# Weights packed on 128 partitions, 29 slots instead of 27 and a fifth kept head in a cached-attention decode kernel

## The chip, the cores and the metric

The kernel runs on one core of a Trainium2 chip. A core has the engines TensorE (PE), VectorE (DVE), ScalarE (ACT), GpSimd (POOL) and SyncE (SP), and 16 DMA engines that move data between HBM and the core's SBUF. The metric is the device time of one execution in microseconds. Before the change it is 1222.26 us, the median of three runs (1220.59 to 1224.09).

## What is computed

Eight batch rows of width 448, one token each, go through two layers. Both layers use the same weights and the same K and V cache. One layer is attention over 4096 cached positions (16 query heads, 8 K/V heads, head size 256), and then a small MLP block. The part of the reference that matters:

```python
def _A_ref(x, k_cache, v_cache, wq, wo):      # B=8, Sq=1, D=448, Hq=16, Hkv=8, Sk=4096, Dh=256
    q = (x @ wq).reshape(B, Sq, Hq, Dh).transpose(0, 2, 1, 3)
    k = jnp.repeat(k_cache, rep, axis=1)      # rep = 2
    v = jnp.repeat(v_cache, rep, axis=1)
    scores = jnp.einsum("bhqd,bhkd->bhqk", q, k) * (Dh ** -0.5)
    o = jnp.einsum("bhqk,bhkd->bhqd", _softmax(scores), v)
    return o.transpose(0, 2, 1, 3).reshape(B, Sq, Hq * Dh) @ wo
...
x = A_x
x = x + _A_ref(_layernorm(x), A_k_cache, A_v_cache, A_wq, A_wo)
x = x + _B_ref(_layernorm(x), B_w1, B_w2, B_w3, B_w4)
x = x + _A_ref(_layernorm(x), A_k_cache, A_v_cache, A_wq, A_wo)
x = x + _B_ref(_layernorm(x), B_w1, B_w2, B_w3, B_w4)
```

With one token, the shifted terms of `_B_ref` are zero, so `w1` and `w2` drop out, and what is left of it is `x1 + gelu(layernorm(x1) @ w3) @ w4`. All inputs are bf16. K and V are 134 MB in total each; K or V of one batch row and one head is 2.1 MB.

## The kernel before

**Pairs.** The work is cut into 128 pairs (layer, batch row, K/V head). One pair takes K (2.1 MB) and V (2.1 MB) of its head. K comes in two runs of 1.05 MB (`K_RUN = 2` chunks each), V in four chunks of 0.52 MB. For a pair, DVE transposes the K runs in place in blocks of 32 by 32 (L548, four per run), PE makes the scores of both query heads from each run (L571), DVE takes the maximum (L578, L580), POOL reduces it over the partitions (L582), ACT makes the exponentials (L588), DVE transposes them (L593), PE multiplies with each V chunk (L610), DVE and PE sort and scale the result (L615, L622, L629), and PE multiplies it with the output weights into `psM` (L640).

**Slots.** K and V live in one SBUF tensor `kv`, cut in `NSLOT = 27` slots of one chunk (128 partitions by 4 KB). A K run takes two adjacent slots, a V chunk one. A slot comes free when PE has read it, and the next load into it waits for that.

**K is used twice.** Both layers need the same K of a batch row. For heads 4 to 7 (`KEEP_RUNS`) the transposed K stays in its slots from layer 0 until layer 1 has used it: 4 heads by 4 slots, 16 slots at the fullest. In layer 1 such a pair loads only V. The other heads (0 to 3) load K in both layers. So 192 K runs and 512 V chunks are loaded.

**Order of the pairs.** Layer 1 of a row can start when layer 0 has ended with the MLP block for it: function `tail` (L658 adds the attention result, then a norm, `w3`, gelu, `w4`, L697, a norm, the query projection at L454, and `expand`, which writes the queries into the tile `qx` at L480). This is the turn of the row. The list `jobs` covers it with other pairs. For a middle row b the order is: layer 0 of heads 4 to 7 of b; layer 1 of heads 0 to 3 of b-1; then `MIX = 1` layer-0 pair of b+1 ahead, and after it layer-1 pairs of b with kept K in turn with further pairs ahead.

**Queues.** All loads are issued by SP in one order: the K runs of pair n, then the V chunks of pair n-1 (`V_LAG = 1`). An issue waits in order: what stands behind a waiting load waits too. The order on PE, DVE, ACT and POOL is found when the program is built: `Graph.schedule` plays the tasks with planned durations, priorities (10 times the pair's number, with small offsets) and the slot pool, and writes down one fixed order for each engine; semaphores guard it. Multi-step DVE work stands as single tasks, so that steps of the norm and gelu in `tail` stand between the transposes of K.

**Weights and x.** `x` is loaded transposed, in pieces of four elements, on 112 partitions (L386). `wq` and `w3` are laid out as 112 partitions by four rows each, since 448 = 112 x 4 (L388, L395), `wo` and `w4` on 128 partitions (L392, L397). `wo`, `w3` and `w4` are issued after the first pairs' loads. Each row's result is stored from `xT` when its layer 1 has ended (L705).

## Time and profile before

The profiled execution took 1223.6 us; its span from the first to the last instruction is 1221.7 us, with a mean granted TensorE clock of 0.541.

| what | before |
|---|---|
| median of three runs | 1222.26 us |
| profiled execution | 1223.6 us |
| its span | 1221.7 us |
| bytes moved by DMA | 483.00 MB, mean 395 GB/s |
| read from HBM | 480.32 MB |
| K loads (1.05 MB) | 192 |
| V loads (0.52 MB) | 512 |
| DVE transposes of K (L548) | 768, mean 690 ns |
| mean granted TensorE clock | 0.541 |

The page of the profile gives each engine's busy time and its share of the span, then the span in 40 equal slices of 30.5 us: a digit is the busy share of an engine in tenths, and the last row is what the DMA engines moved in GB/s. The chain that ended last follows the work back from the last instruction to what released it. A stretch's row begins with its start and end in us. Rows that name an instruction give line, engine, operation, output and inputs. `SPq` stands for SP's queue issuing a load; its length contains the time it waited.

### The profile page before, as it was taken

How to read it: one execution, taken by the hardware profiler on the slowest of the kernel's cores; microseconds unless marked ns; L12 is line 12 of the kernel's file. 1: busy time of each engine (PE TensorE's matmuls, PEld its weight loads, DVE VectorE, ACT ScalarE, POOL GpSimd, SP SyncE). 2: the span in 40 equal slices, each digit the busy share in tenths (PEclk: the TensorE clock that was granted, in tenths of full speed). 3: DMA queues.
4: the chain of work that ended last, by engine and by line, in shares of the span. 5: the costliest groups of instructions: out<-in, count | busy, mean ns of one | idle time of the engine just before them, and what ended most of it. 6: DMA issues, size and time to landing. Idle time of an engine off the chain costs nothing.

```text
span 1221.7 us, 41286 instructions
## 1 busy us (share of the span) xinstructions
PE 727.4 (60%) x18516; PEld 496.0 (41%) x18516; DVE 822.8 (67%) x2683; ACT 118.7 (10%) x305; POOL 99.3 (8%) x272
## 2 busy tenths in 40 slices
PE   2424675567645775467755676556754577545665
PEld 1212454355423553245522454235532355323544
DVE  5627757776677666677667766677667776677763
ACT  0100011011100110000110011000110011100010
POOL 0000000000000000000000001000000001000000
PEclk9755555556555555555555555555565555555555
DMA  9999999999999999999999999999999999999994
GB/s 297 411 343 413 410 410 413 385 404 411 402 415 411 400 398 414 414 397 409 398 414 410 397 411 395 414 408 398 411 387 414 412 395 399 415 414 397 406 397 165
DMA packets 106592, 483.00 MB, mean 395 GB/s; under 512 B 13264, under 2 KB 15056, under 8 KB 81616
## 3 DMA queue, kind: packets, MB, share of 16 engines
q1 hardware_dynamic: 105392, 480.37, 99.1%
q8 instruction: 145, 2.38, 0.8%
q14 instruction: 31, 0.25, 0.1%
q10 hardware_dynamic: 1024, 0.01, 0.0%
HBM read 480.32 MB, written 0.01 MB: 393 GB/s over the span
## 4 chain that ended last, share of the span: by engine, by line
DMA 74%; PE 12%; SPq 6%; DVE 5%; issue 3%; ACT 0%; POOL 0%; ACTq 0%; DVEq 0%
DMA kv<-in_A_v_cache_dram 69%; PE psS L571 5%; SPq L559 4%; PE psO L610 4%; DMA kv<-in_A_k_cache_dram 3%; DMA wo_sb<-in_A_wo_dram 2%; SPq L542 2%; DVE kv L548 2%; PE psX L692 1%; PE psX L667 1%; DVE oT L629 1%; PE psM L640 1%; PE psO L622 0%; DVE oX L615 0%; PE psX L454 0%
## 5 line engine op out<-in xcount | busy, mean ns | idle before, releaser
L548 DVE STREAM_TRANSPOSE kv<-kv 128x512 int32<-128x512 int32 x768 | 498.9, 690 | 55.2 <-DMA kv<-in_A_k_cache_dram 54.0
L610 PE MATMUL psO<-kv,pT 128*2 128x256 bf16 x4096 | 289.7, 397 | 171.7 <-DMA kv<-in_A_v_cache_dram 141.8
L571 PE MATMUL psS<-kv,qx 128*8 128x128 bf16 x8192 | 265.5, 301 | 141.2 <-DVE kv L548 111.2
L571 PEld LDWEIGHTS psS<-kv,qx 128*8 128x8 bf16 x8192 | 210.9, 119 | 172.2 <-DVE kv L548 117.3
L610 PEld LDWEIGHTS psO<-kv,pT 128*2 128x2 bf16 x4096 | 75.2, 90 | 302.1 <-DMA kv<-in_A_v_cache_dram 248.8
L588 ACT ACTIVATE p<-psS,nb 128x256 bf16<-128x256 f32 x128 | 105.6, 834 | 899.7 <-DVE nb L584 856.7
L578 DVE TENSOR_REDUCE pm<-psS 128x1 f32<-128x256 f32 x128 | 53.9, 421 | 111.8 <-PE psS L571 108.2
L640 PE MATMUL psM<-oT,wo_sb 128*128 128x1 bf16 x2048 | 87.4, 173 | 66.1 <-DVE oT L629 53.1
L615 DVE STREAM_TRANSPOSE oX<-psO 128x256 f32<-128x256 f32 x128 | 57.1, 446 | 102.2 <-PE psO L610 101.8
L582 POOL PARTITION_ALL_REDUCE gm<-pmh x128 | 45.5, 355 | 810.2 <-DVE pmh L580 577.0
L640 PEld LDWEIGHTS psM<-oT,wo_sb 128*128 128x128 bf16 x2048 | 77.1, 117 | 82.1 <-DVE oT L629 64.0
L629 DVE TENSOR_SCALAR oT<-psO,rc 64x4 bf16<-64x4 f32 x256 | 55.4, 217 | 32.6 <-PE psO L622 28.0
L597 POOL PARTITION_ALL_REDUCE db<-rsh x128 | 51.0, 399 | 282.5 <-DVE rsh L595 234.6
L593 DVE STREAM_TRANSPOSE pT<-p 128x256 bf16<-128x256 bf16 x128 | 55.7, 436 | 12.3 <-ACT p L588 10.0
L622 PE MATMUL psO<-oX,id 128*32 128x4 f32 x1024 | 37.0, 202 | 44.3 <-DVE oX L615 33.0
L622 PEld LDWEIGHTS psO<-oX,id 128*32 128x32 f32 x1024 | 28.5, 143 | 79.4 <-DVE oX L615 60.5
L584 DVE CUSTOM_DVE_ANT_0 nbx<-gm,ownneg 128x2 f32<-128x2 f32 x128 | 19.1, 149 | 27.8 <-POOL gm L582 26.6
L692 PE MATMUL psX<-hT,w_sb 128*128 128x1 bf16 x896 | 31.7, 171 | 8.4 <-DVE hT L684 6.8
L692 PEld LDWEIGHTS psX<-hT,w_sb 128*128 128x128 bf16 x896 | 30.3, 116 | 10.9 <-DVE hT L684 9.1
L667 PE MATMUL psX<-n,w_sb 112*128 112x1 bf16 x896 | 26.2, 165 | 12.9 <-DVE n L751 12.9
L588 ACT ACTIVATION_READ_ACCUMULATOR p<-psS,nb 128x1 f32 x128 | 33.8, 264 | 0.0
L454 PE MATMUL psX<-n,wq_sb 112*128 112x1 bf16 x1024 | 29.3, 165 | 4.5 <-DVE n L751 3.2
(109 smaller groups left out, 317.1 us busy)
## 6 DMA issues: line engine op xcount, KB each, us to landing
kv<-in_A_v_cache_dram SPq DMA_DIRECT2D x512, 512.0 KB, 15.4
kv<-in_A_k_cache_dram SPq DMA_DIRECT2D x192, 1024.0 KB, 15.5
wq_sb<-in_A_wq_dram SPq DMA_DIRECT2D x1, 3584.0 KB, 17.7
wo_sb<-in_A_wo_dram SPq DMA_DIRECT2D x1, 3584.0 KB, 27.9
w_sb<-in_B_w_dram SPq DMA_DIRECT2D x2, 1568.0 KB, 30.2
out_dram<-xT ACTq DMA_DIRECT2D x8, 0.9 KB
xT<-in_A_x_dram SPq DMA_DIRECT2D x1, 7.0 KB, 2.2
```

Of the source, the lines that this page charges most:

```text
L548: return e.transpose(ap, ap)
L571: last = e.matmul(S[32 * j:32 * j + 8, w * y:w * y + w], qx[x][:, h, 2 * c + u, :], kt[:, :, c, 8 * j:8 * j + 8, u], start=(c == 0 and u = ...
L578: g.add("dve", lambda e: e.tensor_reduce(pm[par][:, :], S[:, 0:256], axis=AX.X, op=ALU.max), 0.44, pr, reads=[rS], writes=[res(f"pm{par}")])
L588: g.add("act", lambda e: e.activation(p_sb[par][:, :].rearrange("p (z k y) -> p y z k", z=8, k=8), S[:, 0:256].rearrange("p (y z k) -> p y ...
L593: g.add("dve", lambda e: e.transpose(pT[par][:, :], p_sb[par][:, :]), 0.44, pr, reads=[rP], writes=[rPT])
L597: g.add("pool", lambda e: e.partition_all_reduce(db[par][:, :], rs2[par][:, :], P, ReduceOp.add), 0.45, pr + 1, reads=[res(f"rsh{par}")], ...
L610: last = e.matmul(O[32 * j:32 * j + 2, 0:DH], pt[:, i, 2 * a:2 * a + 2], slot_ap(vin)[:, i * DH:(i + 1) * DH], start=(a == 0 and i < 4), s ...
L615: g.add("dve", lambda e: e.transpose(oX[par][:, :].rearrange("p (c r) -> p c r", r=32), O[:, 0:DH].rearrange("p (a r k) -> p a k r", a=2, ...
L622: last = e.matmul(O[32 * a:32 * a + 32, 256:260], id4[:, :], oX[par][:, :].rearrange("p (a k r) -> p a k r", a=2, k=4)[:, a % 2, :, a // 2 ...
L629: g.add("dve", lambda e, j=j: e.tensor_scalar(oT[64 * j:64 * j + 64, jb, 4 * h:4 * h + 4], O[64 * j:64 * j + 64, 256:260], rc[par][64 * j: ...
L640: last = e.matmul(psM[layer][:, c:c + 1], wo_sb[:, c0:c0 + 509:4], oT[:, jb, kt_:kt_ + 1], start=(first and k == 0 and c == 0), stop=False ...
L692: last = e.matmul(M[:, 64 + c:65 + c], w4_sb[:, c0:c0 + 509:4], hT[:, ft:ft + 1], start=(ft == 0), stop=(ft == NFT - 1))
```

## The change

- `wq` and `w3` are packed: rows 0 to 383 as three blocks of 128 partitions, and the last 64 rows in two halves of their columns, on partitions 0 to 63 and 64 to 127. Each such tensor is loaded by five transfers instead of one. The normed vectors get a fifth column: the last 64 elements a second time, on the upper partitions. `wo`, `w4` and all vectors go from 112 to 128 partitions, the fourth column filled for 64 partitions only.
- The memory saved, with one `qx` for layer 0 instead of two, and one tile each for `p` and `oX` instead of two, gives `NSLOT = 29`.
- K of five heads (3 to 7) is kept. 176 K runs are loaded.
- `MIX = 2`: at the turn two pairs of the next row come before the first layer-1 pair. With heads 0 to 2 loaded twice, a middle row is: five layer-0 pairs, three layer-1 pairs of the row before, two ahead, one layer-1 pair, one ahead, four layer-1 pairs.
- x is loaded as 8 rows into `wo_sb`, and transposed by four matmuls with an identity `eye`; the load of `wo` waits for these. The results are transposed back in the end by four matmuls, copied by ACT, and stored by one transfer.
- The planned durations become pairs (until a result can be used, and how long the engine is taken), so the fixed orders differ on all engines.

The core of the diff:

```diff
-NSLOT = 27
-KEEP_RUNS = {4: 2, 5: 2, 6: 2, 7: 2}
+NSLOT = 29
+KEEP_RUNS = {3: 2, 4: 2, 5: 2, 6: 2, 7: 2}
...
-MIX = 1
+MIX = 2
...
-BYTES_PER_US = 0.412e6
+V_RATE = 0.4096e6
+K_RATE = 0.4194e6
...
-        self.dur = dur
+        self.dur, self.occ = dur if isinstance(dur, tuple) else (dur, dur)
...
-                        free_at[e] = now + dur
+                        free_at[e] = now + got.occ
...
-    wq_sb = sb("wq_sb", [CP, NCC, HQ * DH], bf)
-    wo_sb = sb("wo_sb", [P, 32 * D + 64], bf)
-    w3_sb = sb("w3_sb", [CP, NCC, F], bf)
-    w4_sb = sb("w4_sb", [P, NFT * D + 64], bf)
+    wq_sb = sb("wq_sb", [P, 7 * HQ * DH // 2], bf)
+    wo_sb = sb("wo_sb", [P, 32 * D], bf)
+    w3_sb = sb("w3_sb", [P, 7 * F // 2], bf)
+    w4_sb = sb("w4_sb", [P, NFT * D], bf)
...
-    qx = [sb(f"qx{i}", [P, HKV, 8, 8], bf) for i in range(4)]
+    qx = [sb(f"qx{i}", [P, HKV, 8, 8], bf) for i in range(3)]
...
-    p_sb = [sb(f"p{i}", [P, 256], bf) for i in range(2)]
+    p_sb = sb("p", [P, 256], bf)
...
-    oX = [sb(f"oX{i}", [P, DH], f32) for i in range(2)]
+    oX = sb("oX", [P, DH], f32)
...
-    dma(lambda e: e.dma_start(xT[:, :, :], A_x[:, 0, :].rearrange("b (p c) -> p b c", c=NCC)),
-        8000, 0, writes=[res("xT")])
-    dma(lambda e: e.dma_start(wq_sb[:, :, :], A_wq.rearrange("(p c) n -> p c n", c=NCC)),
-        D * 4096 * 2, 0, writes=[res("wq")])
+    dma(lambda e: e.dma_start(wo_sb[0:B, 0:D], A_x[:, 0, :]), 8000, 0, writes=[res("wo")])
+
+    def packed(w_sb, w, n, name, queue):
+
+        for c in range(3):
+            dma(lambda e, c=c: e.dma_start(w_sb[:, c * n:(c + 1) * n], w[c * P:(c + 1) * P, :]),
+                P * n * 2, 0, queue, writes=[res(name)])
+        for u in range(2):
+            dma(lambda e, u=u: e.dma_start(w_sb[64 * u:64 * u + 64, 3 * n:3 * n + n // 2],
+                                           w[3 * P:D, u * n // 2:(u + 1) * n // 2]),
+                32 * n * 2, 0, queue, writes=[res(name)])
+
+    packed(wq_sb, A_wq, HQ * DH, "wq", dma_order)
+
+    def xin(e):
+        for c in range(NCC):
+            m = min(P, D - c * P)
+            last = e.matmul(psX[0][0:m, 128 + B * c:128 + B * c + B], wo_sb[0:B, c * P:c * P + m], eye[0:B, 0:B],
+                            start=True, stop=True)
+        return last
+    g.add("pe", xin, 0.5, -5, reads=[res("wo"), res("const")], writes=[res("psX0", True)])
...
-    dma(lambda e: e.dma_start(w3_sb[:, :, :], B_w3.rearrange("(p c) n -> p c n", c=NCC)),
-        D * F * 2, 0, late, writes=[res("w3")])
+    packed(w3_sb, B_w3, F, "w3", late)
...
+    def packed_ap(w_sb, n, c, f, m=P):
+
+        if c < 3:
+            return w_sb[:, c * n + f:c * n + f + m], c
+        u = f // (n // 2)
+        f = 3 * n + f - u * n // 2
+        return w_sb[:, f:f + m], 3 + u
...
-        x = 2 * layer + b % 2
+        x = layer + layer * (b % 2)
...
-        ops.append(lambda e: e.tensor_scalar(dsts[-1], xc[:, :, :], y[:, k - 1:k], None, ALU.mult))
-        g.add("dve", ops, 0.205 * len(ops), prio, reads=[rM, rL], writes=[rL, dst_res])
+        ops.append(lambda e: e.tensor_scalar(dsts[-1][:, :, 0:4], xc[:, :, :], y[:, k - 1:k], None, ALU.mult))
+        ops.append(lambda e: e.tensor_copy(dsts[-1][64:128, :, 4:5], dsts[-1][0:64, :, 3:4]))
+        g.add("dve", ops, (0.21, 0.12), prio, reads=[rM, rL], writes=[rL, dst_res])
...
-        else:
-            g.add("act", lambda e: ("dma", e.dma_start(
-                out[b, 0, :].rearrange("(p c) -> p c", c=NCC), xT[:, b, :])), 0.1, prio, reads=[nx2])
...
+    def xout(e):
+        for c in range(NCC):
+            m = min(P, D - c * P)
+            last = e.matmul(psX[0][0:B, 64 + c * P:64 + c * P + m], xT[0:m, :, c], eye[0:m, 0:m],
+                            start=True, stop=True)
+        return last
+    g.add("pe", xout, 0.5, -1, reads=[res(f"xT{b}") for b in range(B)] + [res("const")], writes=[rM])
+    g.add("act", lambda e: e.copy(wq_sb[0:B, 0:D], psX[0][0:B, 64:64 + D]), 0.6, -1, reads=[rM], writes=[res("wq")])
+    g.add("act", lambda e: ("dma", e.dma_start(out[:, 0, :], wq_sb[0:B, 0:D])), 0.1, -1, reads=[res("wq")])
```

## The prediction, made before the changed kernel had run

> **What bounds the kernel now.** I read the page first: busy time, the slices, the chain, the transfers.
>
> ```profile
> PE 727.4 (60%) x18516; PEld 496.0 (41%) x18516; DVE 822.8 (67%) x2683; ACT 118.7 (10%) x305; POOL 99.3 (8%) x272
> ...
> DMA  9999999999999999999999999999999999999994
> GB/s 297 411 343 413 410 410 413 385 404 411 402 415 411 400 398 414 414 397 409 398 414 410 397 411 395 414 408 398 411 387 414 412 395 399 415 414 397 406 397 165
> ...
> DMA 74%; PE 12%; SPq 6%; DVE 5%; issue 3%; ACT 0%; POOL 0%; ACTq 0%; DVEq 0%
> ...
> kv<-in_A_v_cache_dram SPq DMA_DIRECT2D x512, 512.0 KB, 15.4
> kv<-in_A_k_cache_dram SPq DMA_DIRECT2D x192, 1024.0 KB, 15.5
> ```
>
> No engine is busy for more than 67%, the DMA engines are busy in every slice but the last, and three quarters of the chain are transfers. Second, stages, as stretches of the trace (first busy times by engine; the last two numbers are the busy share of the DMA engines and what they moved in GB/s):
>
> ```profile
> 0.00:10.00 10.00, 0.00 (x0) 0.00 (x0) 3.20 (x11) 0.00 (x0) 1.03 (x8) 1.00 0.90 204
> 10.00:20.00 10.00, 1.62 (x25) 1.47 (x26) 3.81 (x23) 0.00 (x0) 1.92 (x8) 1.00 0.92 267
> 60.00:70.00 10.00, 1.73 (x48) 1.65 (x48) 0.00 (x0) 0.00 (x0) 0.00 (x0) 0.50 1.04 259
> 70.00:80.00 10.00, 0.00 (x0) 0.00 (x0) 0.00 (x0) 0.00 (x0) 0.00 (x0) 0.50 1.05 350
> ...
> 230.00:240.00 10.00, 5.75 (x130) 3.79 (x125) 7.10 (x26) 0.83 (x2) 0.75 (x2) 0.50 0.94 368
> 240.00:250.00 10.00, 5.21 (x140) 3.66 (x136) 7.90 (x33) 0.83 (x2) 0.75 (x2) 0.50 0.96 370
> 530.00:560.00 30.00, 20.19 (x535) 14.80 (x524) 23.39 (x90) 2.71 (x7) 2.09 (x6) 0.50 1.01 398
> 1060.00:1070.00 10.00, 5.07 (x120) 2.88 (x120) 7.07 (x19) 0.83 (x2) 0.75 (x2) 0.50 1.02 413
> 1205.00:1221.00 16.00, 6.25 (x150) 5.26 (x150) 5.38 (x30) 0.21 (x1) 0.00 (x0) 0.50 0.01 2
> ```
>
> 413 GB/s (1060 to 1070) is the rate at which DMA is full. The reader is to see four places below it: the start, while wq_sb loads; 60 to 80, while wo_sb and w3_sb load; small dips where pairs stream K and V with few slots (230 to 250, 530 to 560); and 16 us at the end with hardly any transfer. The work list is therefore: bytes, the two weight stages, the dips, the end.
>
> **The change, part by part.** Sums stand against the profiled execution, 1223.6 us (span 1221.7, 1.9 around it), which lies 1.3 above the runs' median of 1222.26.
>
> *K of five heads kept.* Layer 1 reads one more head of K from SBUF in each of 8 batches: 8 x 2 runs of 1.049 MB are not loaded, 16.8 MB of 480. At 413 GB/s that is 40.6 us. With them go 16 x 4 transposes of 690 ns (L548), 44 us of an engine that isn't the bound: nothing.
>
> *Weights on 128 partitions.* Two loads over 112 partitions are slow. From 0 to 20 the DMA moved 204 and 267, 4.7 MB; at 413 from the first byte at 2 us it would be 7.4: 2.7 MB, 6.6 us. From 60 to 80 it moved 6.1 MB instead of 8.3: 5.2 us. The packed loads have forms whose rate the trace has: 128 partitions x 8 KB is K's own form. New are four pieces on 64 partitions, 0.75 MB together. Their price lies between full rate, 1.8 us, and the 112-partition rate of about 210 (60 to 80 less its full-rate part), 3.6 us; I take the slow end, since half the partitions are nearest to that row: 1.8 us lost. Sum 6.6 + 5.2 - 1.8 = 10 saved, bounds 7 and 12. The Trainium skill has a rule against these pieces: SBUF — State Buffer, Door 1: The DMA port swizzle (why `[64,N]` ≈ `[32,N]`) says that 64 adjacent partitions reach half of the 16 ports, 196 GB/s measured there; an estimate from it is 3.8 us for the pieces. No run here shows a 64-partition load yet; by the rule the sum is 0.2 lower, by full rate 1.8 higher.
>
> *x as rows, transposed on PE.* Before the first norm come four matmuls, two copies and, within it, one more DVE step: some 0.5 + 2 x 0.2 + 0.2, and POOL's identity 0.5 later: the first scores, at 29.2 now, come 2 us later. Cover: 28 slots can fill before any is reused, 28 x 0.524 MB / 0.413 = 35 us of transfers after wq_sb, then 16 us of weights. Without it: 2 us. The load of wo_sb waits for those matmuls, near 17 us; queued behind it on SP are w3_sb, w4_sb and K of pair 4, all of which reach the DMA only after 45 us. Nothing.
>
> *Two heads ahead at the turn; one qx, p and oX less.* From the last layer-0 head of a batch to the layer-1 queries the trace has 39 us:
>
> ```profile
> 964.09 0.16 DVE L658 TENSOR_TENSOR xT<-psM,xT 112x4 bf16<-112x4 f32 x1
> ...
> 1003.44 0.29 DVE L480 CAST qx<-psX 32x128 bf16<-32x128 f32 x1
> ```
>
> A pair with K and V is 4.19 MB, 10.1 us. Before, four pairs of layer 1 and one ahead cover it (51 us); now three and two: the same. Shared p and oX wait for the transpose or matmul of the pair before, under 1 us of work in a 5 us pair: nothing, at most a share of the next part.
>
> *Fewer free slots.* This is the cost. Kept K fills 20 of 29 slots: 9 are left where 11 of 27 were. Nine hold the run of K being read (2), its second run (2) and V of the pair before (4). So, in the order of the changed program, the next pair's first run waits for this pair's first scores, with 6 chunks of 0.524 MB queued behind the landing; before, 8. How long that wait is the trace shows (start, length):
>
> ```profile
> 524.38 6.34 SPq L542 DMA_DIRECT2D kv<-in_A_k_cache_dram  x2
> ...
> 526.21 0.70 DVE L548 STREAM_TRANSPOSE kv<-kv 128x512 int32<-128x512 int32 x1
> ...
> 529.31 1.02 PE L571 MATMUL psS<-kv,qx 128*8 128x128 bf16 x32
> ```
>
> K lands, DVE starts at 526.2, PE's scores end at 530.3, SP has issued at 530.7: 4.5 us. Six chunks last 6 x 1.27 = 7.6 us, so 3.1 remain queued when the new load is issued; eight left 5.6. What a load needs before it moves at rate is the fastest landing less its own bytes: 5.5 - 2.5 = 3.0 us.
>
> ```profile
> DMA to landing us min/median/max: 5.5/15.5/31.7
> ```
>
> 3.1 against 3.0: on the edge. Behind the waiting K run SP holds V of this pair and all that follows, and PE waits for that V. Price of a pair: with 5.6 left, 530 to 560 moved 398 for 413, 1.1 us for three pairs, 0.4 each; 230 to 250, where K was issued late with three chunks left, lost (1 - 369/413) x 20 = 2.1 us for two pairs, 1.1 each. The second row is the nearer: 0.7 more per pair. There are 4 such successions of K and V pairs in each of six batches, 2 in the first and 5 in the last: 31 x 0.7 = 22 us. Ends: 0, if 3.1 us suffice, and 45, at twice the row.
>
> *End.* From the last layer's L658 to the last step the chain runs without transfers:
>
> ```profile
> 1208.08 0.17 DVE xT L658
> ...
> 1218.25 0.16 DVE xT L697
> ```
>
> The change adds the shifted copy in the norm (0.2), four matmuls (0.4) and ACT's copy of 8 x 448 from PSUM; ACT's 128 x 256 takes 0.83, a 32 x 128 copy 0.26: 0.6 to 1.2. One store of 8 rows takes the place of the last of eight; the other seven were hidden. Sum +1.5, ends 0.8 and 2.5.
>
> Sum: 1223.6 - 40.6 - 10 + 1.5 + 22 = 1196.5 in the profiled execution; 1.3 less against the median: **1195**.
>
> **The rivals.** *Transfers stay back to back.* For it: 28 slots at the start, deep queues (median 15.5 us to landing) in most of a batch, and in 160 to 180, with V alone, full rate too. Then the slot term is 0 to 8, middle 5: 1178. Against it: 3.1 us on the edge of 3.0, and the dips that 11 slots show already.
>
> *A new wait, slower than before.* In the changed order, DVE takes the norm and gelu steps of the tail between the four transposes of a K run; in the worst pair eleven stand there. At about 0.19 each the answer of 4.5 us becomes 6.6, and one chunk is left where three are needed: 2.1 us idle on top of 0.7. If it were so in all 31 successions, the slot term would be 87 us and the time 1260; in half of them 54 us and 1227. It decides from 49 us of slot loss, 1.6 per succession. For it: DVE is 7 to 8 of 10 us busy in these stretches. Against: only one of four successions of a batch has that many steps between; the others have three or four.
>
> *The weights stay slow.* If the 112 partitions were not the reason for 204 to 267 GB/s (both loads also have 14 to 32 KB runs, and the start has the 8-byte pieces of x), the 10 us stay away: 1205. Against: the piece of the trace with w4_sb, 128 partitions in 896 B rows, ends the dip.
>
> **How the numbers follow.** Forecast (slots on the edge, 1186 to 1206) 0.50; transfers back to back (1172 to 1186) 0.25; weights stay slow or twice the slot loss (1206 to 1218) 0.12; slower 0.10, no change 0.03. The range leaves out the slower tail and a little below: 1174 to 1214. A difference under 0.3%, some 3.7 us, can't be told from none with this kernel; faster by more 0.87, within 0.03, slower 0.10.
>
> **What would show it.** K loads 176 instead of 192 and the first 20 us above 350 GB/s: bytes and weights right. Slices of the steady part between 385 and 400 where pairs stream K and V, and SP's waits for psS (L571 of before) longer than now: slot term right; slices at 410: the first rival. First scores near 31 us with no dip at 45 to 60: start right. More than 18 us between the last transfer and the end, or V-only stretches under 395, would show a cost that isn't in the sum; so would a slot loss outside the successions named.

## The result, and the profile after

The changed kernel takes 1212.14 us (median of four runs, 1210.78 to 1214.98) where the kernel before took 1222.58 beside it: a ratio of 0.9919, 95% interval 0.9894 to 0.9944. The prediction was 1195, so 10 us of the 27 that were forecast came; the time lies near the upper end of the stated range, 1174 to 1214. Run once more on another chip, the changed kernel took 1210.62 against 1218.66 there, a ratio of 0.9942 (0.9914 to 0.9970). The profiled execution took 1213.35 us, its span is 1211.6.

The page of the changed kernel: busy times, the rate in 40 slices, the chain by engine, and the K and V loads.

```profile
PE 785.4 (65%) x18524; PEld 561.2 (46%) x18524; DVE 801.3 (66%) x2654; ACT 120.3 (10%) x306; POOL 100.5 (8%) x274
...
GB/s 349 409 392 411 399 392 413 404 384 384 413 414 389 343 400 413 413 349 367 411 414 388 377 394 410 414 392 372 394 411 414 396 369 392 414 414 372 272 409 125
...
DMA 42%; PE 31%; DVE 17%; issue 6%; ACT 2%; SPq 1%; POOL 1%; ACTq 0%; POOLq 0%; DVEq 0%
...
kv<-in_A_v_cache_dram SPq DMA_DIRECT2D x512, 512.0 KB, 13.8
kv<-in_A_k_cache_dram SPq DMA_DIRECT2D x176, 1024.0 KB, 14.9
```

Sixteen K runs are gone, as planned. But the slices that stood at 385 to 415 now fall to 343, 349, 367 and once to 272, and the share of the chain that is transfers fell from 74% to 42%. (That share alone does not name the bound: slots_32 below, the fastest kernel of all, has 16%.) TensorE, which has the same work, is busy for 58 us more; that comes up again below.

Stretches of the changed kernel (busy times of PE, its weight loads, DVE, ACT, POOL; then clock, busy share of DMA, GB/s):

```profile
0.00:10.00 10.00, 0.00 (x0) 0.00 (x0) 3.04 (x18) 0.00 (x0) 1.21 (x9) 1.00 0.79 300
10.00:20.00 10.00, 1.55 (x8) 1.28 (x8) 2.25 (x15) 0.00 (x0) 2.22 (x9) 1.00 1.02 333
...
60.00:70.00 10.00, 3.83 (x48) 3.41 (x48) 0.00 (x0) 0.00 (x0) 0.00 (x0) 1.00 1.08 344
70.00:80.00 10.00, 3.78 (x96) 2.07 (x96) 5.78 (x12) 0.00 (x0) 0.36 (x1) 1.00 1.02 414
250.00:290.00 40.00, 31.78 (x823) 25.17 (x819) 28.77 (x113) 4.08 (x11) 3.03 (x8) 0.54 0.98 372
...
740.00:760.00 20.00, 13.76 (x320) 9.54 (x320) 11.14 (x34) 2.00 (x6) 1.91 (x5) 0.61 1.02 414
1100.00:1150.00 50.00, 31.91 (x726) 22.18 (x726) 34.76 (x136) 4.08 (x11) 3.06 (x8) 0.50 0.82 312
...
1191.00:1211.00 20.00, 10.37 (x206) 7.90 (x202) 6.49 (x34) 0.74 (x2) 0.00 (x0) 0.50 0.01 5
```

The start moves more than before (204 and 267 then), and so does the stage of `w3` (259 and 350 then). A stretch where pairs stream K and V, 250 to 290, stands at 372 (408 before), and 1100 to 1150, the last turn, at 312 (399 before). Full rate, 414, is still there at 740 to 760. The same two stretches in the kernel before:

```profile
250.00:290.00 40.00, 29.23 (x788) 21.27 (x792) 27.10 (x106) 4.10 (x11) 3.01 (x8) 0.54 1.02 408
...
1100.00:1150.00 50.00, 32.08 (x804) 22.28 (x808) 37.46 (x129) 4.05 (x11) 3.01 (x8) 0.50 1.00 399
```

**Where the time went.** The trace has the landing of every load. With deep queues, two K runs land 2.50 us apart and two V chunks 1.275 us (medians of each trace, within 0.01 wherever K comes in runs of two chunks). These distances, times 192 or 176 runs and 512 chunks, are the transfers' own time. What successive landings lie further apart than that, summed up, I call the excess. The rest is the start with the weights, and what follows the last landing. The four add up to the span:

| us | before | after | difference | forecast |
|---|---|---|---|---|
| K and V, own time | 1133.2 | 1093.2 | -40.0 | -40.6 |
| start and weights | 41.2 | 33.6 | -7.6 | -10 |
| excess | 30.9 | 65.4 | +34.5 | +22 |
| after the last landing | 16.4 | 19.4 | +3.0 | +1.5 |
| span | 1221.7 | 1211.6 | -10.1 | -27.1 |

So the bytes came out as worked out, and 12.5 of the 17 us that are missing are excess. By blocks of 16 pairs the excess was 3.4, 4.3, 3.8, 4.6, 3.7, 4.5, 3.5, 3.2 before, and is 4.2, 7.2, 8.5, 10.0, 6.8, 7.2, 7.7, 14.0 after: 1 to 5 more in every block, and 11 more in the last. The second profile of the changed kernel has an excess of 61.0; it is from a chip on which the kernel before is 4 us faster too, and that kernel has no profile there. A median that is off by 0.003 us moves the sum over 512 V chunks by 1.5 us, so an excess is good to some 3 us.

Two things stand out beside it. First, K's loads wait longer for scores. SP's waits by line, in the kernel before (us in total, times, longest):

```profile
SPq L542 <- PE psS L571: 156.0, 57, 9.4
...
SPq L559 <- PE psX L472: 11.5, 4, 5.6
```

and in the changed kernel:

```profile
SPq L573 <- PE psS L602: 188.8, 46, 6.9
...
SPq L590 <- PE psX L505: 41.9, 11, 6.3
```

K runs (L573, L542 before) wait for scores 46 times instead of 57, but 4.1 us each instead of 2.7. V chunks (L590, L559 before) wait 41.9 us instead of 11.5 behind the matmuls that write out a turn's queries (L505, L472 before); all 11 of these waits lie before 1095, none in the last turn. A wait of SP is not yet a loss, since the loads issued before it still run: K's waits for the PV matmuls (L641, L610 before) fell at the same time, from 207.1 to 111.1.

Second, the output projection, which the diff doesn't touch in count, got slow. The group in the kernel before, with the busy time and mean ns of one after the bar:

```profile
L640 PE MATMUL psM<-oT,wo_sb 128*128 128x1 bf16 x2048 | 87.4, 173 | 66.1 <-DVE oT L629 53.1 <-DMA wo_sb<-in_A_wo_dram 10.1 <-issue 2.6
```

The same work after, in its two forms, weights of 128 and of 64 columns, and both together (they overlap, and the row names the more frequent form):

```profile
L672 PE MATMUL psM<-oT,wo_sb 128*128 128x1 bf16 x1536 | 121.8, 171 | 64.7 <-DVE oT L660 59.0 <-issue 2.5 <-DMA wo_sb<-in_A_wo_dram 2.5
...
L672 PE MATMUL psM<-oT,wo_sb 128*64 128x1 bf16 x512 | 105.7, 206 | 0.0
...
L672 PE MATMUL psM<-oT,wo_sb 128*128 128x1 bf16 (+1 forms) x2048 | 165.7, 180 | 64.7 <-DVE oT L660 59.0
```

That is 165.7 us instead of 87.4, or 1.29 us per pair instead of 0.68. Three candidates, then, for the excess: the slots, the last turn, and this.

### The profile page after: what moved, and what is told of

Its sections match the earlier page's. It is cut to its first block, busy times and chain, and to the rows that moved or that the text cites. A ratio compares the mean times of both kernels' runs of the same rounds, so it can differ in the third digit from the quotient of the medians.

```text
span 1211.6 us, 41233 instructions
## 1 busy us (share of the span) xinstructions
PE 785.4 (65%) x18524; PEld 561.2 (46%) x18524; DVE 801.3 (66%) x2654; ACT 120.3 (10%) x306; POOL 100.5 (8%) x274
## 4 chain that ended last, share of the span: by engine, by line
DMA 42%; PE 31%; DVE 17%; issue 6%; ACT 2%; SPq 1%; POOL 1%; ACTq 0%; POOLq 0%; DVEq 0%
DMA kv<-in_A_v_cache_dram 35%; DVE kv L579 9%; PE psS L602 9%; PE psO L641 8%; PE psM L672 6%; DMA kv<-in_A_k_cache_dram 5%; PE psX L726 3%; DMA wo_sb<-in_A_wo_dram 2%; PE psX L488 2%; DVE oT L660 2%; ACT p L619 1%; DVE pm L609 1%; PE psO L653 1%; DVE oX L646 1%; DVE pT L624 1%
## 5 line engine op out<-in xcount | busy, mean ns | idle before, releaser
L579 DVE STREAM_TRANSPOSE kv<-kv 128x512 int32<-128x512 int32 x704 | 453.3, 687 | 49.8 <-DMA kv<-in_A_k_cache_dram 47.7
L641 PE MATMUL psO<-kv,pT 128*2 128x256 bf16 x4096 | 280.4, 396 | 88.0 <-DMA kv<-in_A_v_cache_dram 75.1
L602 PEld LDWEIGHTS psS<-kv,qx 128*8 128x8 bf16 x8192 | 202.7, 116 | 188.4 <-DVE kv L579 117.0
L672 PE MATMUL psM<-oT,wo_sb 128*128 128x1 bf16 (+1 forms) x2048 | 165.7, 180 | 64.7 <-DVE oT L660 59.0
L672 PEld LDWEIGHTS psM<-oT,wo_sb 128*128 128x128 bf16 (+1 forms) x2048 | 141.8, 110 | 97.9 <-DVE oT L660 75.8
L641 PEld LDWEIGHTS psO<-kv,pT 128*2 128x2 bf16 x4096 | 93.8, 100 | 179.7 <-DMA kv<-in_A_v_cache_dram 141.2
L653 PEld LDWEIGHTS psO<-oX,id 128*32 128x32 f32 x1024 | 26.7, 138 | 96.3 <-DVE oX L646 80.3
L726 PE MATMUL psX<-hT,w_sb 128*128 128x1 bf16 (+1 forms) x896 | 33.3, 171 | 11.8 <-issue 6.7
L726 PEld LDWEIGHTS psX<-hT,w_sb 128*128 128x128 bf16 (+1 forms) x896 | 31.2, 113 | 17.8 <-issue 9.1
L630 DVE RECIPROCAL rc<-db 128x2 f32<-128x2 f32 x128 | 19.1, 149 | 19.4 <-POOL db L628 19.3
L611 DVE TENSOR_SCALAR pmh<-cap,pm 128x2 f32<-128x2 f32 x128 | 29.0, 227 | 3.3
```

The lines of the kernel that those rows point to most:

```text
L579: return e.transpose(ap, ap)
L602: last = e.matmul(S[32 * j:32 * j + 8, w * y:w * y + w], qx[x][:, h, 2 * c + u, :], kt[:, :, c, 8 * j:8 * j + 8, u], start=(c == 0 and u = ...
L641: last = e.matmul(O[32 * j:32 * j + 2, 0:DH], pt[:, i, 2 * a:2 * a + 2], slot_ap(vin)[:, i * DH:(i + 1) * DH], start=(a == 0 and i < 4), s ...
L653: last = e.matmul(O[32 * a:32 * a + 32, 256:260], id4[:, :], oX[:, :].rearrange("p (a k r) -> p a k r", a=2, k=4)[:, a % 2, :, a // 2], st ...
L672: last = e.matmul(psM[layer][0:m, c:c + 1], wo_sb[:, c0:c0 + m], oT[:, jb, kt_:kt_ + 1], start=(first and k == 0 and c == 0), stop=False, ...
L726: last = e.matmul(M[0:m, 64 + c:65 + c], w4_sb[:, c0:c0 + m], hT[:, ft:ft + 1], start=(ft == 0), stop=(ft == NFT - 1))
```

## The experiments

The kernel before, run beside every set, has medians from 1217.95 to 1218.67 in the five sets (1222.58 beside the result above), so times of different sets can stand beside each other. Where a difference to the changed kernel is given, it is to the 1210.62 of its run in the fourth set.

### The last turn, the output projection, three more slots, four heads

**turn_2**: one pair less behind the last turn.

```diff
         jobs += [(0, b, h) for h in range(HKV) if h in KEEP_RUNS]
-        if b:
+        if b == B - 1:
+            jobs.insert(len(jobs) - 1, (1, b - 1, tail_heads[0]))
+            jobs += [(1, b - 1, h) for h in tail_heads[1:]]
+        elif b:
             jobs += [(1, b - 1, h) for h in tail_heads]
```

> The changed kernel with one pair moved in the list of the last batch: (layer 1, batch 6, head 0) stands before the last layer-0 pair of batch 7 instead of behind it, so that two pairs (20 us of transfers) instead of three (30 us) stand between that pair and the first pair that needs batch 7's layer-1 queries, which come about 40 us later. Bytes, slots and all else are the same. Last-turn theory (of the 10 us that the changed kernel came out above what bytes, weights and slots give, most is idle DMA while this turn lasts): one pair less of cover, 8 to 11 us more, about 1222. Slots-alone theory (the loss is spread over all successions of K and V pairs): the same number of successions, 1212 within 2. Slow-output-matmul theory (L672 takes 1.27 us per pair instead of 0.68): 1212 within 2.

Measured: 1215.04 (10 runs, 1210.83 to 1220.02), ratio 0.9978 (0.9964 to 0.9992), 4 to 7 us above the changed kernel. The trace has the place. In the changed kernel the last row's turn runs from L690 to the last copy of the queries:

```profile
1101.33 0.16 DVE L690 TENSOR_TENSOR xT<-psM,xT 128x4 bf16<-128x4 f32 x1 [0.35 <-PE psM L672]
...
1141.29 0.29 DVE L513 CAST qx<-psX 32x128 bf16<-32x128 f32 x1
```

That is 40 us, and behind it stand only the three pairs (1, 6, 0 to 2), 30 us of transfers: in the last row nothing is left to be worked on ahead. What follows needs these queries. SP's wait for the scores of the first such pair, number 120, in 1130 to 1160 of the changed kernel:

```profile
SPq L590 <- PE psS L602: 12.6, 4, 8.2
```

and in turn_2:

```profile
SPq L593 <- PE psS L605: 17.0, 3, 13.7
```

The longest wait is now 13.7 us instead of 8.2. The excess at the landings of pair 120's V is 4.0 us in the changed kernel (4.9 in its second profile), 13.4 in turn_2, and below 0.3 before. So the last turn's loss exists, 4 to 5 us; that it would be most of the miss is refuted.

**wo_cols**: the output projection's loops exchanged.

```diff
-            for k in range(4):
-                kt_ = 4 * h + k
-                for c in range(NCC):
+            for c in range(NCC):
+                for k in range(4):
+                    kt_ = 4 * h + k
```

> The changed kernel with the two loops of the output projection (L668, L669) exchanged: 128-column weights for 12 matmuls in a row, then 64-column weights for 4, instead of three of the one and one of the other in turn. Same matmuls, same count. If the alternation is what makes them slow, L672's busy time falls from 165.7 to about 90 us, and V-only stretches (405 GB/s in 1160 to 1190) go to 412. Slow-output-matmul theory: it lengthens the answer to a landing, so 10 to 25 us of the slot loss and 3 us of the end come back: 1187 to 1202. Last-turn and slots theories: only the end and the V-only stretches gain, 3 to 6 us: 1206 to 1209.

Measured: 1210.37 (1203.15 to 1215.29), ratio 0.9929 (0.9906 to 0.9952): no difference that stands out of the scatter. The two forms in wo_cols, and both together:

```profile
L672 PE MATMUL psM<-oT,wo_sb 128*128 128x1 bf16 x1536 | 60.5, 166 | 63.7 <-DVE oT L660 60.5 <-DMA wo_sb<-in_A_wo_dram 2.5
...
L672 PE MATMUL psM<-oT,wo_sb 128*64 128x1 bf16 x512 | 45.8, 192 | 4.0 <-issue 4.0
...
L672 PE MATMUL psM<-oT,wo_sb 128*128 128x1 bf16 (+1 forms) x2048 | 97.1, 173 | 67.7 <-DVE oT L660 60.5 <-issue 4.0 <-DMA wo_sb<-in_A_wo_dram 2.5
```

They take 97.1 us instead of 165.7. In the kernel before the loops stand in the order of the changed kernel, with 128 columns throughout, and take 87.4: so it is the alternation of the two widths that slowed them. The excess stays at 65.0, and the V-only stretch 1160 to 1190 has 400 GB/s, not the 412 expected. The theory of the slow output matmul is refuted; only the time after the last landing is shorter, 18.0 instead of 19.4, and turn_2, whose output projection is that of the changed kernel, has 18.0 as well.

**slots_32**: three more slots, in the room of the second MLP weight.

```diff
-NSLOT = 29
+NSLOT = 32
...
-    w4_sb = sb("w4_sb", [P, NFT * D], bf)
+    w4_sb = w3_sb
...
-    dma(lambda e: e.dma_start(w4_sb[:, 0:NFT * D].rearrange("p (t n) -> p t n", n=D),
-                              B_w4.rearrange("(t m) n -> m t n", m=P)),
-        D * F * 2, 0, late, writes=[res("w4")])
```

> The changed kernel with 32 slots instead of 29, 12 free of kept K instead of 9. The room comes from the second MLP weight: it isn't loaded (1.6 MB, 3.9 us less at 413 GB/s), and its matmuls read the first MLP weight's tile in the same number and shapes, so the output is another. Slot theory with my sizes: the loss of about 26 us in the batches between goes down to some 4, and three more slots hold 3.8 us more of transfers in the last turn: 1212 - 4 - 22 - 4 = 1182, within 6. Slots-alone theory, with all of the last stretch's loss too: 1172 to 1176. Slow-output-matmul theory (the answer itself is too long): 1212 - 4 = 1208 to 1200.

Measured: 1171.67 (1171.18 to 1172.03), ratio 0.9615 (0.9602 to 0.9627). That is 39 us below the changed kernel; the load that is left out is 3.9 of it by its bytes, and the control slots_29 below, which leaves it out in 29 slots, is 1.8 us below the changed kernel. The excess is 26.7 instead of 65.4, with 4.5 in the last block: all the growth since the kernel before goes with three slots, the last turn's part too. What else the change brought, the shared p and oX, `MIX = 2`, the new planned durations and the slow output projection, is in slots_32 as well, so none of it costs excess by itself when the slots are there.

**keep_4**: four kept heads in 29 slots (`KEEP_RUNS` without head 3, `MIX = 1`).

> The changed kernel with K of four heads kept and one head ahead at the turn, as before, in its 29 slots: 13 free instead of 9, 16.8 MB more, and four pairs instead of three behind the last turn. Bytes +40.1 us. Slot and last-turn theories: -26 and -10, so about 1216 (1212 to 1220), and the excess of the transfers over their own bytes is 32 us or less, as before. Slow-output-matmul theory: it would be lost here too, as L672 is still slow: 1235 to 1248.

Measured: 1212.79, ratio 0.9955 (0.9942 to 0.9968). The excess is 26.3 at 13 free slots, 35 to 39 less than in the two profiles of the changed kernel, which pays for nearly all of the 40 us of bytes. The slow output projection is in this kernel too, and nothing of it shows in the excess.

### What a slot is worth

**slots_29** and **slots_30** are slots_32 with that number, **slots_28** is the changed kernel with 28 (`NSLOT` alone).

> The control for the kernel with 32 slots: 29 slots as in the changed kernel, the second MLP weight not loaded and the first one's tile read in its place. Both theories: 1.6 MB less, the changed kernel less 3 to 5 us; in ratio to the kernel before 0.988 to 0.990. If it fell by 10 or more, the load itself, not the slots, would explain a part of what 32 slots gave.

> The same with 30 slots, 10 free. Edge theory (the next pair's first K run has 6 chunks queued behind its releaser, the answer of 4.5 to 5.3 us and 3 us of start leave it just short; a seventh chunk adds 1.27 us, more than the some 1.1 us lost per succession): 25 to 33 of the 33 us that three slots gave come with the first, so 25 to 33 below the run with 29. Rival, each slot worth the same: 11 below.

> The changed kernel with 28 slots, 8 free. Odd-slot theory (a K run needs two adjacent slots, so the ninth free slot lets no run in earlier, and with 8 the same 6 chunks stand behind the landing that a run waits for): 0 to 6 us more, ratio 0.991 to 0.997. Rival, the loss follows the number of chunks in flight, one less everywhere: at 31 successions 1.27 us each, some 35 to 40 more, ratio 1.020 to 1.025.

| free slots | kernel | us | ratio, 95% | excess |
|---|---|---|---|---|
| 8 | slots_28 | 1224.99 | 1.0054 (1.0037 to 1.0071) | 73.7 |
| 9 | changed kernel | 1210.62 | 0.9942 (0.9914 to 0.9970) | 61.0 |
| 9 | slots_29, without the load of `w4` | 1208.85 | 0.9922 (0.9896 to 0.9948) | 63.5 |
| 10 | slots_30, likewise | 1182.46 | 0.9707 (0.9689 to 0.9724) | 38.3 |
| 12 | slots_32, likewise | 1171.67 | 0.9615 (0.9602 to 0.9627) | 26.7 |

The tenth slot alone gives 26 us, the next two 11 together. The fixed orders are found anew for each number of slots, so a changed order would be a rival; but the K and V loads stand in the same order in all five kernels of the table, and from 29 to 30 and from 30 to 32 slots the sequence of lines on DVE and PE changes in some 1 to 2% only. The price is uneven, as the edge theory expected. A reason for it can be counted in the order of the loads, but no run shows it by itself: with 10 free slots both runs of this pair, V of the pair before and the next pair's first run (2 + 2 + 4 + 2) fit at once, so that the load which waits next has eight chunks behind its releaser instead of six. The odd-slot theory for 28 fell between its rivals: 14 us, neither 0 to 6 nor 35 to 40. The rate in 40 slices with 28 slots:

```profile
GB/s 339 410 395 409 375 378 414 403 364 375 412 414 390 359 408 414 414 375 343 410 413 399 381 358 411 413 394 363 370 411 414 383 342 404 414 414 388 260 409 129
```

with 30, and the chain:

```profile
GB/s 334 411 396 414 409 397 414 413 404 407 413 414 393 404 409 413 409 397 371 411 414 400 411 377 411 414 397 407 389 412 414 391 401 407 414 414 390 311 408 106
...
PE 32%; DMA 31%; DVE 25%; issue 7%; ACT 2%; POOL 1%; SPq 1%; ACTq 0%; POOLq 0%; DVEq 0%
```

with 32:

```profile
GB/s 334 411 396 412 410 412 413 412 408 400 412 414 411 394 404 415 414 410 402 410 414 414 404 396 411 414 411 406 401 412 414 411 401 404 414 414 414 353 409 77
...
DVE 34%; PE 32%; DMA 16%; issue 7%; SPq 5%; ACT 4%; POOL 1%; ACTq 0%; POOLq 0%; DVEq 0%
```

Between the first slice and the last four, the lowest is 342 with 28 slots, 371 with 30 and 394 with 32. At the same time the share of transfers in the chain falls to 16%, while the rate is at its best: with the slots there, the chain runs mostly over steps of DVE and PE.

### Giving a slot back in bytes

**keep_45** keeps one run of head 3 (`KEEP_RUNS` 3: 1), **keep_475** three of its four chunks, the second run loaded as two chunks; 11 and 10 free slots.

> The changed kernel with both runs of four heads and one run of the fifth kept: 18 slots kept, 11 free as before the change, 8.4 MB more than the changed kernel. Edge theory: bytes +20, slot loss -33: 13 below the changed kernel, ratio 0.978 to 0.984. Rival, each slot worth 11 us: 20 - 22, ratio 0.989 to 0.992.

> The changed kernel with three of the four K chunks of head 3 kept instead of four: 19 slots kept, 10 free, 4.2 MB more than the changed kernel. Head 3's second run is loaded as two single chunks with 64-column score matmuls. Edge theory: bytes +10, the tenth free slot -26: 16 below the changed kernel, ratio 0.976 to 0.982. Rival, each slot worth 11 us: -1, ratio 0.990 to 0.993.

Measured: keep_45 1203.18, ratio 0.9870 (0.9855 to 0.9885); keep_475 1201.93, ratio 0.9858 (0.9841 to 0.9874). They are 7 and 9 us faster than the changed kernel, and both lie between the two expectations. Their excess is 37.8 and 45.8, with 10.2 and 10.6 of it in the last block; keep_4, with four pairs behind the last turn and 13 free slots, has 3.7 there.

### The last turn covered

**cover_4**: K of head 3 of row 6 isn't kept, and its pair stands behind the last turn.

```diff
             jobs += [(1, b - 1, h) for h in tail_heads]
+        if b == B - 1:
+            jobs += [(1, b - 1, 3)]
...
-        again = [(1, b, h) for h in keep_heads]
+        again = [(1, b, h) for h in keep_heads if b != B - 2 or h != 3]
...
-                keep = layer == 0 and y // K_RUN >= fresh
+                keep = layer == 0 and y // K_RUN >= fresh and (b != B - 2 or h != 3)
```

> The changed kernel, but in batch 6 K of head 3 isn't kept: it is loaded again (2.1 MB, 5 us), and its layer-1 pair stands as a fourth one behind the last turn; in batch 6 13 slots are free. Last-turn theory (with three pairs this turn leaves the DMA idle for some 7 us): bytes +5, turn -7, slots in batch 6 -3 to -5: 4 to 8 below the changed kernel, ratio 0.985 to 0.989. Rival (the last stretch loses by its slots alone): +5 - 4, ratio 0.991 to 0.995.

Measured: 1208.86 (1206.61 to 1215.52), ratio 0.9928 (0.9908 to 0.9948): the 5 us of bytes are won back and no more. The excess at pair 120's V is gone (below 0.3), and the block of row 6 falls to 3.8, but the block of the last pairs still has 10.9 (the profiled execution, 1215.52, is the longest of the eight). My 7 us for the turn was too much; 4 to 5 is what the landings show.

### Shorter and longer answers

**run_1**: K in runs of one chunk (`K_RUN = 1`, kept runs 4 per head).

> The changed kernel with K loaded in runs of one chunk instead of two; slots, kept heads and bytes as they are. A run now answers after two transposes and half the matmuls (some 1.8 us sooner), and its one slot comes back by itself, so that 8 chunks instead of 6 stand behind the landing that the next pair's K waits for. Edge theory: the slot loss of 33 to 36 us goes, 352 K chunks at 1.275 us instead of 2.50 per two cost 8 us: 24 to 28 below the changed kernel, ratio to before 0.969 to 0.973. Rival (128 score matmuls of 64 columns per pair instead of 64 of 128 make TensorE's answer longer, or the chunk rate is worse): same as the changed kernel or slower, 0.99 to 1.00.

Measured: 1320.59, ratio 1.0838 (1.0820 to 1.0856), far outside both. TensorE's waits for nothing that the profile shows ("issue") in run_1, and the packets that carry instructions:

```profile
PE psS L602 <- issue: 145.9, 79, 4.3
```

```profile
q8 instruction: 209, 3.42, 1.0%
```

In the changed kernel the two rows are

```profile
PE psS L602 <- issue: 20.8, 16, 2.0
```

```profile
q8 instruction: 145, 2.38, 0.8%
```

Runs of one chunk take 8,192 more score matmuls, with their weight loads 16,384 more instructions. They came in 64 more packets of 16 KB, and TensorE stood for up to 4.3 us at a time, 125 us more in all, where nothing that the profile shows held it. The likely reading, not tested by itself, is that its code came late. The experiment says nothing of the answer.

**half_runs**: each run by two DMAs into the same two slots, matmuls as they were; **room_half** is the same on the kernel with 30 slots below.

```diff
-                dma(lambda e, kin=kin, y=y: e.dma_start(slot_ap(kin[0], K_RUN), k_run(b, h, y, K_RUN)),
-                    K_RUN * P * CHUNK * 2, pr, kq[n], writes=[rk], takes=kin)
+                for z in range(K_RUN):
+                    t = dma(lambda e, kin=kin, y=y, z=z: e.dma_start(
+                        kv[:, (kin[0].slot + z) * CHUNK:(kin[0].slot + z + 1) * CHUNK], k_run(b, h, y + z, 1)),
+                        P * CHUNK * 2, pr, kq[n], writes=[rks[z]], takes=() if z else kin)
...
-                    g.add("dve", tr, (0.75, 0.615), pr + 4, reads=[rk], writes=[rKT])
+                    g.add("dve", tr, (0.75, 0.615), pr + 4, reads=[rks[hf // 2]], writes=[rKT])
```

> The changed kernel with each K run loaded by two DMAs of one chunk into the same two adjacent slots; transposes 1 and 2 wait for the first, 3 and 4 for the second; matmuls, slots and kept heads as they are. After the last landing of a run only two transposes are left instead of four, 1.3 us less, with the number of slots unchanged. Answer theory (what counts is the time from a landing to the next issue against the chunks queued behind it): 1.3 us are worth a chunk, 16 to 26 us by the runs with 28 and 30 slots; K's chunks cost 352 x 0.027 = 9.5: 7 to 17 below the changed kernel, ratio 0.978 to 0.986. Rival (the number of slots alone counts): 9 above it, ratio 0.997 to 1.001.

> The same on the kernel with 30 slots and the whole computation. There the transfers' excess is 43 us where 29 are left at 12 free slots, so 14 us at most are to be had, and the chunks cost 9.5: 1187 to 1196, ratio 0.974 to 0.982.

Measured: half_runs 1215.59, ratio 0.9975 (0.9962 to 0.9988); room_half 1216.65, ratio 0.9974 (0.9961 to 0.9987). At 29 slots the excess fell from 61.0 to 53.0, but the own time rose by 12.1, most of it since K's chunks now land 1.280 us apart instead of 1.25; at 30 slots the excess rose as well, from 40.8 to 48.4, so that room_half is 25 us slower than room_30. The time of half_runs lies in the rival's range (0.997 to 1.001), that of room_half outside the one stated for it: the shorter answer gave 8 us at most, and the split cost more. The answer theory is not confirmed.

**late_answer** and **late_answer_32**: six matmuls that nobody reads ahead of the first run's scores, in the changed kernel and in slots_32.

```diff
             def sc(e, kin=kin, y=y):
                 last = None
+                if y == 0 and (layer == 0 or h in tail_heads):
+                    for _ in range(6):
+                        e.matmul(S[0:8, 256:512], qx[x][:, h, 0, :], slot_ap(kin[0])[:, 0:256],
+                                 start=False, stop=False, skip_group_check=True)
```

> The changed kernel with six more matmuls (8 x 256 outputs that nobody reads) ahead of the first run's score matmuls of the 88 pairs that load that run: its slots come back later by what the six take (1 to 1.5 us by their neighbours on TensorE), with bytes, slots, DVE and the order unchanged. Answer theory: as one chunk less in the queue, 16 us (28 against 29 slots) to 26 us (29 against 30) more than the changed kernel, ratio 1.007 to 1.016. Rival (the number of free slots alone counts): 0 to 3 more, ratio 0.993 to 0.997.

> The same six matmuls in the kernel with 32 slots and without the second MLP weight's load, as the control: with 12 free slots a later answer is covered, 0 to 4 us above that kernel's 0.9615, ratio 0.961 to 0.965. If the matmuls cost their own time on TensorE, 10 to 25 us would come here too.

Measured: late_answer 1245.90, ratio 1.0222 (1.0191 to 1.0254), 35 us above the changed kernel; late_answer_32 1201.64, ratio 0.9863 (0.9847 to 0.9880), 30 us above slots_32. The six matmuls in late_answer, and its busy times:

```profile
L600 PE MATMUL psS<-kv,qx 128*8 128x256 bf16 x528 | 123.8, 404 | 120.1 <-DVE kv L579 89.9 <-DVE g L714 18.2 <-DVE st_0c L782 7.2
```

```profile
PE 834.8 (67%) x19052; PEld 638.1 (52%) x19052; DVE 798.8 (65%) x2654; ACT 120.3 (10%) x306; POOL 100.5 (8%) x274
```

and the chain of late_answer_32:

```profile
PE 52%; DVE 28%; issue 8%; DMA 6%; ACT 4%; POOL 2%; ACTq 0%; POOLq 0%; SPq 0%; DVEq 0%
```

They take 1.41 us per pair (123.8 over 88 pairs); TensorE as a whole is busy for 49 us longer and still for 67% alone, and the loss is again in the transfers: the excess grows from 61.0 to 90.8 and from 26.7 to 57.1. So later scores cost time, and in the changed kernel somewhat more than a slot does, as the answer theory says. But the control failed: 12 free slots, which the theory took for enough, lose nearly as much, more than the 10 to 25 us that its expectation gave for the matmuls' own time on TensorE. In late_answer_32 the chain has 6% of transfers and 52% of PE left, and a landed K run waits 5.2 us in the mean for its first transpose (3.0 in slots_32, 0.9 in the changed kernel): the data lie ready and the engines come late. The pair of runs therefore doesn't separate a later answer from more work on TensorE. That slots and answers trade against each other one for one, and that there is a number of chunks from which all is covered, is not shown.

### A version that beats both

**room_30** finds 4 KB per partition among the small tiles, so that the whole computation has 30 slots.

```diff
-NSLOT = 29
+NSLOT = 30
...
-    qx = [sb(f"qx{i}", [P, HKV, 8, 8], bf) for i in range(3)]
+    qx = [sb(f"qx{i}", [P, HKV, 8, 8], bf) for i in range(2)]
...
-    pT = [sb(f"pT{i}", [P, 256], bf) for i in range(2)]
+    pT = [sb("pT", [P, 256], bf)] * 2
...
-    eye = sb("eye", [P, P], bf)
+    eye = w4_sb[:, 0:P]
+    eye2 = wq_sb[:, 1024:1024 + P]
```

> The whole computation in 30 slots, 10 free with five heads kept. The 4 KB per partition come from small tiles: one pT instead of two; two qx instead of three (layer 1's next queries are copied after the last pair that reads the old ones); the first norm's temporaries lie in oX; the identity lies in w4_sb's place at the start and in wq_sb's at the end; the narrow tiles lie side by side in one. Edge theory: what the 30th slot gave without the second MLP weight (26 us) is had here too, less what sharing costs: ratio to before 0.970 to 0.977, 1182 to 1190. Rival (one pT and two qx put a wait in the slot's place): 0.985 to 0.995.

Measured: 1191.70, ratio 0.9776 (0.9759 to 0.9793): 19 us below the changed kernel, just above what was expected (0.977). The excess is 40.8, near the 38.3 of slots_30: sharing the tiles doesn't put a wait in the slot's place.

**room_cover_wo** adds to it the edits of cover_4 and wo_cols.

> The kernel with 30 slots and the whole computation, with the fourth pair behind the last turn (K of head 3 of batch 6 loaded again, +5 us; the wait of pair 120's V, 5.6 us, gone; 14 free slots in batch 6, -1 to -2) and the output projection's loops exchanged (the last pairs' TensorE work shorter, -1 to -3 at the end). 1186 to 1191, ratio 0.973 to 0.977.

Measured: 1188.90 (1187.91 to 1191.18), ratio 0.9754 (0.9737 to 0.9771), the lowest time of the whole computation, though its interval overlaps that of room_30. Its last block has an excess of 4.2 instead of 10.7 in room_30, the kernel as a whole 36.7 instead of 40.8; against that stand 5 us of bytes more. So the wait in the last turn is gone, but that the edits pay for their bytes is not shown. The rate in slices:

```profile
GB/s 335 410 391 413 412 405 412 414 402 395 411 414 384 388 406 414 414 385 387 411 414 392 390 377 411 413 392 404 389 411 414 414 411 411 413 413 385 378 407 127
```

The slice of the last turn, 272 in the changed kernel, is at 378, and the lowest of the others between the first and the last is 377.

**after_again** is the changed kernel once more, in the fourth set.

> The changed kernel itself once more, beside the three others, for their differences on one chip: ratio 0.989 to 0.995.

Measured: 1210.62 (1207.72 to 1216.23), ratio 0.9942, as used above.

## Why the prediction was right or wrong

**Bytes, -40.6: right.** 16 runs, 40.0 us of own time.

**Weights, -10 (7 to 12): right within its bounds, -7.6.** The first 20 us moved 300 and 333 GB/s, not the 350 that I named as the sign, so that sign failed. The four pieces on 64 partitions were priced at the slow end, 3.6 us for 0.754 MB. `wq`'s two landed in 2.40 us and `w3`'s in 1.09, 3.49 together or 216 GB/s by the distances of their landings, which hold neighbouring transfers too. The Trainium skill (SBUF — State Buffer, Door 1: The DMA port swizzle) gives 196 GB/s measured at 1 MiB for partitions 0 to 63; these smaller pieces come out 10% above it here. So the slow end was the right one for them. What was missing is elsewhere: `wq`'s third piece of 1.05 MB landed 4.1 us after the second instead of 2.5.

**x as rows, nothing: right.** The first scores start at 30.5 instead of 29.2, and 20 to 60 runs at 410.

**Two heads ahead at the turn, nothing: wrong in the last row.** The prediction counted five pairs behind the turn, "now three and two: the same". That holds for the rows 1 to 6. In rows 0 and 7 one of the two kinds is missing, and the count goes from four to three. In row 0 the turn takes 30 us (124.9 to 154.5) and three are enough; in row 7 it takes 40, over 30 us of transfers. It cost 4 to 5 us, shown by the landings of pair 120, by turn_2 (13.4) and by cover_4 (none). The sharing of p and oX wasn't tried by itself; slots_32 has it too, at an excess of 26.7.

**Fewer free slots, +22: the failed step, by its size.** The excess grew by 34.5, of which 4.0 is the turn: 30.5 for the slots where 22 were forecast (25 with the second profile). That slots are the cause is shown by slots_28, slots_30 and slots_32, with slots_29 as their control, and by keep_4. The working had two rows, 1.1 us per succession with late K and 0.4 for the pairs of the kernel before, and took the difference, 0.7 times 31. The 0.4 was no loss by slots: the excess of the kernel before is 30.9, and with 12 or 13 free slots it is still 26.7 and 26.3. At most 4.6 us of it were a price for 11 slots, where 31 times 0.4, some 12, were subtracted. Without the subtraction the same row gives 34; that this is near 30.5 is partly luck, since the row was one stretch of 20 us and the price of a slot is anything but even. The threshold behind it, 3.1 us left against 3.0 needed, isn't what the runs show either: one slot less costs 14 us, one more gives 26, and six more matmuls ahead of the scores cost 35 at 9 and 30 at 12 free slots. Why the price is so uneven stays open. The signs named for the slot term came: slices under 400 where pairs stream K and V, and longer waits of K's loads for scores.

**End, +1.5: came out at +3.0, for another reason.** From L690 to the end it is 13.6 us in both kernels, so the priced copy, matmuls and store add nothing that shows. The extra lies before it, and with 19.4 us the sign for a cost that isn't in the sum (more than 18) came. The changed kernel after its last landing at 1192.2:

```profile
1193.76 1.45 PE L641 MATMUL psO<-kv,pT 128*2 128x256 bf16 x24
1195.27 0.45 DVE L646 STREAM_TRANSPOSE oX<-psO 128x256 f32<-128x256 f32 x1 [2.81 <-PE psO L641]
...
1196.66 1.32 PE L672 MATMUL psM<-oT,wo_sb 128*128 128x1 bf16 x16 [0.60 <-DVE oT L660]
1198.02 0.16 DVE L690 TENSOR_TENSOR xT<-psM,xT 128x4 bf16<-128x4 f32 x1 [1.41 <-PE psM L672]
```

TensorE takes up the last PV matmuls 1.56 us after the landing, because the output projection of the pair before stands ahead of them, 1.32 us as well; then it does 24 of them in 1.45 us, where the kernel before had 8 left, in 0.60; and the last output projection takes 1.32 us instead of some 0.68. These three make up the 3.0. Only the last, 0.6 us, is the alternation for certain: in turn_2, with the same projection, the PV matmuls begin 0.2 us after the last landing, and the whole is 18.0, as in wo_cols. The prediction had left this edit out: it saw that padding went away, but not that 128- and 64-column weights then alternate. For the time as a whole it hardly matters.

**The rivals.** Transfers back to back, 1178, is nearly what 12 free slots give (1171.7, and 3.9 for the load left out), but not 9. The slower rival, steps of the tail between the transposes, didn't come true: from the first start to the last end the four transposes of a K run take 2.84 us in the mean, where the kernel before takes 3.05. That later scores would cost, late_answer shows, 35 us for 1.4 us per pair, though not whether by the wait or by TensorE's time. The measured 1212 lies in the stretch (1206 to 1218, chance 0.12) of "weights stay slow or twice the slot loss": the weights did not stay slow, and the slot loss was 1.4 times the forecast.

## What to carry to other kernels

When kept data takes slots from a stream, measure the loss at full stream and at a larger pool first; a dip in the profile may have other causes, and subtracting it as already paid makes the price too low (here 22 us instead of 34, with 30.5 measured). Count cover for the last round by itself, where nothing is left to work on ahead. Before a whole buffer's worth of bytes is traded for a slot, look for the slot among the small tiles: here 4 KB per partition were worth 19 us, almost half of the fifth head's K.

## What the runs showed of the hardware

- Alternating weights of 128 and 64 columns (three and one) makes 16 matmuls take 1.29 us instead of 0.68; with 12 and 4 in a row it is 0.76 (97.1 us over 128 pairs).
- With 209 instruction packets instead of 145, TensorE had 146 us of waits instead of 21 in front of score matmuls for which the profile shows no releaser (run_1), and the kernel became 110 us slower. The Trainium skill (Runtime: NRT & Kernel Launch, Instruction fetch mechanics) calls the cost of crossing a 16 KiB boundary of the code mostly hidden; if these waits are code that came late beside full DMA queues, it was not hidden here.
- The same K lands at 1.280 us per chunk in DMAs of 0.52 MB (half_runs) and at 1.25 in DMAs of 1.05 MB, some 10.6 us over 352 chunks.
- The scatter of the runs differs between kernels: the changed kernel from 1207.7 to 1216.2 in five runs, wo_cols from 1203.2 to 1215.3 in six, but slots_32 from 1171.2 to 1172.0 in four. Few slots alone aren't the reason: slots_28, with the fewest, stayed within 1223.3 to 1227.1 in four.
